# A head over four feature tiles, TensorE without waits for itself, and new paces in a planned attention and feed-forward kernel

## The chip, the cores and the metric

The kernel runs on one core of a Trainium2 chip, as one program. The metric is the time of an execution in microseconds (us); the time of a kernel is the median of its runs. A core has five engines that run beside each other, each through its own instructions in order, with semaphores between them: TensorE (PE) multiplies matrices, VectorE (DVE), ScalarE (ACT) and GpSimd (POOL) do the element work, and SyncE (SP) issues nearly all the DMAs. TensorE writes to PSUM, which has eight banks; one bank holds 128 x 512 values in float32. Everything else is kept in SBUF.

## The reference, cut to what matters

There are 2048 tokens of 640 features. A linear attention with 32 heads of 20 features and a gated feed-forward layer of 1728 hidden features see the same input, and a gate per token mixes them. All inputs are bfloat16.

```python
x = A_x                                        # 1 x 2048 x 640
g = sigmoid((x * gate_w).sum(-1))              # one number per token
q, k, v = heads(x @ wqkv)                      # 32 heads of 20
pq, pk = q @ w_phi, k @ w_phi                  # per head, 20 x 20
phi_q = concat(softmax(pq), softmax(-pq))      # 40 features
phi_k = concat(softmax(pk), softmax(-pk))
kv, z = phi_k.T @ v, phi_k.sum(tokens)
a = ((phi_q @ kv) / (phi_q @ z + 1e-6)) @ wo
b = (silu(x @ w_gate) * (x @ w_up)) @ w_down
out = g * a + (1 - g) * b
```

## The kernel before

**The work.** x is loaded transposed (xT, five chunks of 128 features by 2048 tokens), 512 tokens at a time (bt 0 to 3). The hidden features of the feed-forward layer are cut into 14 tiles of 128 (the last has 64). A gate tile (L658) or up tile (L659) for 512 tokens is five matmuls of 512 columns, one for each chunk, summed in one bank. What follows a pair is `ffn_tail` (L617): ACT takes a tanh of the gate bank into hT and copies the up bank into `us`; DVE combines tanh and gate bank (L636), which frees that bank; POOL multiplies by `us` (L642), of which there are three buffers. hT has two buffers, for bt even and odd. `down` (L744) multiplies 14 tiles of hT by w_down for 128 tokens.

For the attention, `premult` (L766) multiplies w_phi into the q and k weights on TensorE, from block-diagonal weights that POOL builds out of phi's weights (L563 to L574). `features` (L828) makes pq or pk for 128 tokens (ten matmuls into a pair of banks). DVE then takes maxima (L859) and minima (L863), subtracts both (L867, L871; the second one frees the pair), ACT takes the exponential, DVE sums (L882) and inverts (L886), and POOL normalizes (L892). A K tile and its v tile go into `kvpart` (L904) when four K tiles are normalized. Q tiles come after, each with a DMA transpose, a product with kv (`num`), a division, another DMA transpose and the product with wo. `finish` and `finals` (L706, L716) mix both results, and SP writes them out.

**What sets the order.** All of it is entered as tasks in a planner (`_Plan`, L230) that runs when the program is built. A task has an engine, an estimated cost, tasks that it depends on, a rank (`prio`), and banks or buffers that it takes and gives back. The planner simulates the engines: whenever one is free, it takes the task of the lowest rank whose dependencies are done by its estimates, whose buffers are free and whose `hold` time has passed. `after` keeps a task behind another one. A load has a `land` time, its expected landing. The order so found is written into each engine's instructions and does not change when the kernel runs. `K_AT + K_EACH * t` and `Q_AT + Q_EACH * t` are the hold times of the K and Q feature tiles (L840), `PRE_AT` that of the first premultiplication, and `K_PAIRS` tells for how many feature tiles bt 0 and bt 1 take turns in the ranking (L1012).

**Semaphores.** `_Tracker.run` (L161) knows for each tile of SBUF and each PSUM bank the last write and the reads since, and `_emit_waits` (L132) makes the engine wait for those that the new instruction conflicts with, unless they are known to be done. Each task's matmuls count one up on TensorE's own semaphore; a conflict of a matmul with an earlier matmul's write to the same bank is treated like any other, so TensorE waits for its own semaphore.

**The head.** `ffn_head` (L665) starts the feed-forward tiles of bt 0 while their data still comes in. It handles HD = 3 tiles: gate for chunks 0-1, up for chunks 0-1, gate for chunks 2-3, gate for chunk 4 (three tiles in each), and up for chunks 2-4, tile by tile. So six banks are in use. The weights for it come in four loads (`load_head`, L525), between those of x: gate chunks 0-1, x chunks 0-1, up chunks 0-1, gate chunks 2-4, x chunks 2-3, x chunk 4, up chunks 2-4 (L529 to L534). Further weights come in column pieces (`PIECES`, L492). Ahead of the head stands one warm-up task (L596): ten matmuls of 512 and two of 128 columns over all eight banks, whose results nobody reads.

Of the kernel before, what the change touches and what calls it, by code (L numbers as in the profile page):

```python
# [6 lines left out]
P = 128  # L7
# [29 lines left out]
class _Tracker:  # L37
# [94 lines left out]
    def _emit_waits(self, eng, need):  # L132
        kn = self.known[eng]
        eobj = self.engobj[eng]
        while True:
            pending = [(s, v) for s, v in need.items() if v > kn.get(s, 0)]
            if not pending:
                return
            s, v = pending[0]
            eobj.wait_ge(self.sem[s], v)  # L140
            self.nwaits += 1
            if v > kn.get(s, 0):
                kn[s] = v
            snap = self._snap(s, v)
            for s2, v2 in snap.items():
                if v2 > kn.get(s2, 0):
                    kn[s2] = v2
# [13 lines left out]
    def run(self, eng, fn, reads=(), writes=(), semname=None, inc=None):  # L161
        rkeys = [self._key_of(a) for a in reads]
        wkeys = [self._key_of(a) for a in writes]
        need = {}

        def req(ev):
            if ev is None:
                return
            s, v = ev
            if v > need.get(s, 0):  # L170
                need[s] = v

        for k in rkeys:
            for kk in self._conflicts(k):
                req(self.lastw[kk])
        for k in wkeys:
            for kk in self._conflicts(k):
                req(self.lastw[kk])
                for s, v in self.readers[kk].items():
                    req((s, v))  # L180
        self._emit_waits(eng, need)
        ins = fn()
        if semname is None:
            semname = {"pe": "pe", "act": "act", "dve": "dve", "pool": "pool"}[eng]
            if inc is None:
                inc = 1
        elif semname == "dma":
            semname = self.new_dma_sem()
            inc = 16
        ins.then_inc(self.sem[semname], inc)  # L190
        self.cnt[semname] += inc
        v = self.cnt[semname]
        ev = (semname, v)
        snapd = dict(self.known[eng])
        if snapd.get(semname, 0) < v:
            snapd[semname] = v
        self.evknow.setdefault(semname, {})[v] = snapd
        for k in wkeys:
            self.lastw[k] = ev
            self.readers[k] = {}  # L200
        for k in rkeys:
            r = self.readers[k]
            if r.get(semname, 0) < v:
                r[semname] = v
        return ev
# [21 lines left out]
        self.slack = 0.0  # L227


class _Plan:  # L230


# [9 lines left out]
    def add(self, eng, cost, fn, deps=(), prio=5.0, lat=None, acq=(), rel=(), name=""):  # L242
        t = _Task(eng, cost, fn, deps, prio, self.LAT[eng] if lat is None else lat,
                  tuple(acq), tuple(rel), len(self.tasks), name)
        self.tasks.append(t)
        return t
# [86 lines left out]
def _build(  # L333
# [9 lines left out]
    gate_w: bass.AP,  # L343
    out: bass.AP,
):
    tr = _Tracker(nc)
    pe, act, dve, pool, sp = nc.tensor, nc.scalar, nc.vector, nc.gpsimd, nc.sync
    run = tr.run

# [51 lines left out]
    wph = sbat("wph", [P, 5, DH], BF16, base + 10 * D * 2 + 5 * 8 * DH * 2)  # L401

    ps = nc.alloc_psum_tensor("ps", [P, 8 * 512], F32)
# [6 lines left out]
    add = plan.add  # L410
# [4 lines left out]
    def one(b, c0, c1, r0=0, r1=P):  # L415
        return ps[r0:r1, b * 512 + c0:b * 512 + c1]
# [62 lines left out]
    def load(eng, dst, src, land, prio, transpose=False, name="load", cost=0.06):  # L479

        t = add(eng, cost, lambda: dma(eng, dst, src, transpose=transpose), prio=prio, lat=2.0, name=name)
        t.land = land
        t.slack = L_SLACK if land > 13 else 0.0
        t.after = chain.get(eng)
        chain[eng] = t
        return t

    def rows(a):
        return a.rearrange("(c p) j -> p c j", p=P)
    gsrc = rows(B_w_gate)  # L490
    usrc = rows(B_w_up)
    PIECES = ((0, 384), (384, 640), (640, 896), (896, 1280), (1280, 1664))  # L492
    NPC = len(PIECES)
    wgl = [None] * (NPC + 1)
    wul = [None] * (NPC + 1)

    def load_gu(j, eng, land, prio):
        c0, c1 = PIECES[j]
        wgl[j] = load(eng, wg[:, :, c0:c1], gsrc[:, :, c0:c1], land[0], prio)
        wul[j] = load(eng, wu[:, :, c0:c1], usrc[:, :, c0:c1], land[1], prio + 0.1)  # L500

    def load_x(bt, prio, *cuts):

        tok = slice(512 * bt, 512 * bt + 512)
        out_ = []
        for i, (c0, c1, land) in enumerate(cuts):
            out_ += [load("sp", xT[:, c0:c1, tok], x2[tok, c0 * P:c1 * P], land, prio + 0.1 * i, True, "x%d" % bt)] * (c1 - c0)
        return out_

    def load_wT(which, land, prio):  # L510
        o = 5 * which
        return load("sp", wqT[:, o:o + 5, :], A_wqkv[:, which * D:(which + 1) * D], land, prio, True, "wT")
# [6 lines left out]
    gw_l = add("act", 0.5, load_gate, prio=-7, lat=6.0, name="gw")  # L519
    gw_l.hold = 11.0  # L520
    xs = [None] * NBT
    HD = 3
    hw = {}

    def load_head(key, c0, c1, land, prio):  # L525
        w, src = (wg, gsrc) if key == "g" else (wu, usrc)
        hw[key, c0] = load("sp", w[:, c0:c1, 0:HD * P], src[:, c0:c1, 0:HD * P], land, prio)
        return hw[key, c0]
    load_head("g", 0, 2, 3.7, -43)  # L529
    xa = load_x(0, -42, (0, 2, 5.2))  # L530
    load_head("u", 0, 2, 6.0, -41)
    wgl[0] = load_head("g", 2, 5, 7.1, -40.5)
    xs[0] = xa + load_x(0, -40, (2, 4, 8.0), (4, 5, 8.6))
    wul[0] = load_head("u", 2, 5, 9.9, -39)  # L534
    load_gu(1, "sp", (11.2, 12.4), -37)
    ph_l = load("sp", wph[:, :, :], rows(A_w_phi.rearrange("h e f -> (h e) f")), 12.6, -36.5)
    load_gu(2, "sp", (13.8, 15.0), -36)
    xs[1] = load_x(1, -35, (0, 5, 17.5))
    wkT_l = load_wT(1, 20.8, -34)
    load_gu(3, "sp", (22.8, 24.4), -33)  # L540
    wv_l = load("sp", wvg[:, :, 0:D], rows(A_wqkv[:, 2 * D:3 * D]), 27.3, -32)
    xs[2] = load_x(2, -31, (0, 5, 31.0))
    load_gu(4, "sp", (32.4, 33.9), -30)
# [44 lines left out]

    WARM = 10
    wctx = {}

    ones_row = nc.const_aps.tensor(1.0, (P, 512), BF16)

    def warm():  # L596
        def fn():
            for i, n in enumerate([512] * WARM + [P] * 2):
                last = pe.matmul(one(i % 8, 0, n), lhsT=ones_row[:, 0:P], rhs=ones_row[:, 0:n], start=True, stop=True, skip_group_check=True)  # L599
            return last  # L600
        run("pe", fn, reads=[], writes=[ps[:, :]])
    warm_t = add("pe", 0.427 * WARM + 0.2, warm, prio=-10, acq=[("bank", wctx, i) for i in range(8)],
                 rel=[("bank", wctx, i) for i in range(8)], name="warm")


    gate_t = {}
# [3 lines left out]
    def w_dep(k):  # L610
        col = P * k
        for j, (c0, c1) in enumerate(PIECES):
            if col < c1:
# [51 lines left out]
    def ffn_head():  # L665
        tsl = slice(0, 512)
        cs = [{} for _ in range(HD)]
        before = warm_t
        last = {}

        def group(key, c0, c1, by_k=False):
            nonlocal before
            w = wg if key == "g" else wu

            def fn(ks, cc):
                mms([(one(cs[k][key], 0, 512), w[:, c, P * k:P * k + P], xT[:, c, tsl], c == 0, c == 4) for c in cc for k in ks])
            for ks in [(k,) for k in range(HD)] if by_k else [range(HD)]:
                t = add("pe", _mm(*[512] * (len(ks) * (c1 - c0))), lambda ks=ks: fn(ks, range(c0, c1)),
                        deps=[xs[0][c1 - 1], hw[key, min(c0, 2)]], prio=-5,
                        acq=[("bank", cs[k], key) for k in ks] if c0 == 0 else (), name="head")  # L680
                t.after = before
                before = t
                for k in ks:
                    last[key, k] = t
        group("g", 0, 2)
        group("u", 0, 2)
        group("g", 2, 4)
        group("g", 4, 5)
        group("u", 2, 5, by_k=True)
        for k in range(HD):  # L690
            ffn_tail(0, k, cs[k], (last["g", k], last["u", k]), 0)

    B_FIRST = 8
    K_AT, K_EACH, Q_AT, Q_EACH = 29.0, 6.10, 122.4, 7.91
    PRE_Q = 10.08
    PRE_EACH = 2.2
    PRE_AT = 23.7
    D_AFTER = 4
    FIN_DVE = 12
    K_PAIRS = 8  # L700
    store_t = {}
    gs_t = {}
    pend = []
# [297 lines left out]

    pre_k = premult(1, wkT_l, 2.0, at=PRE_AT)
    pre_q = premult(0, wqT_l, PRE_Q, 0.02)
    wq_done[0] = pre_q[-1]
# [9 lines left out]
    for bt in range(1, NBT):  # L1014
        ks = list(range(K_PAIRS if bt == 1 else 0, NK))
# [72 lines left out]
```

## Time and profile before

| | us |
|---|---|
| median of 3 runs | 288.47 |
| lowest, highest | 288.34, 288.76 |
| the profiled execution | 288.7 |
| its span, first to last instruction | 286.9 |
| PE busy | 281.3 |
| DVE busy | 224.0 |
| POOL busy | 171.1 |
| ACT busy | 145.5 |

All rows of the profile come from the one profiled execution, and their times count from the start of its span. The part of its time outside the span is 1.8 us. In a timeline a row is: start, duration, engine, line, operation, tiles (out<-in), shapes, number of instructions, and in brackets the idle time before and what ended it. Matmuls overlap, since each is drawn until its result is out; the spacing of their starts is what the array takes. PEld are the weight loads that belong to the matmuls. All matmuls but the warm-up have line 435 (a helper), so they are told apart by their tiles: wg is gate, wu up, wqk features, wd down. Some matmul records, a few per cent, are missing from the trace. In the view by stretches a row is: start:end, length, busy time and number of instructions of each engine, the granted TensorE clock, the busy share of the DMA engines and the GB/s that they moved.

### The profile page before, as it was taken

The page shows a single profiled execution, that of the slowest core. Times are in us where ns is not written, and L with a number is a line of the kernel's source. Part 1 is how long each engine was busy: PE and PEld are TensorE (multiplying, and loading weights), DVE is VectorE, ACT ScalarE, POOL GpSimd, SP SyncE. Part 2 cuts the span into 40 slices and gives each one's busy share as a digit, 9 for nine tenths or more (in the row PEclk, how much of TensorE's full clock was granted, in tenths as well). Part 3 has the DMA queues.
Part 4 walks back from the last instruction along what each step waited for, and adds up shares of the span by engine and source line. Part 5 has one row for each costly group of instructions (what it writes and reads, how often), then busy time and mean ns, then how long its engine had stood idle before and what let it go on. Part 6 is the DMA issues. An engine that isn't in the chain of part 4 may idle for free.

```text
span 286.9 us, 5145 instructions
## 1 busy us (share of the span) xinstructions
PE 281.3 (98%) x2014; PEld 151.1 (53%) x2052; DVE 224.0 (78%) x318; ACT 145.5 (51%) x222; POOL 171.1 (60%) x164
## 2 busy tenths in 40 slices
PE   8999999999999999999999999999999999999996
PEld 3344555546555545555555555555455565455654
DVE  1233379999999999989999987989999978962212
ACT  2437648676664774445463534456665544562210
POOL 5199305787378656763685566676986666665100
DMA  7999999100000000000118426544346335223211
GB/s 149 265 214 268 258 190 357 58 1 3 0 0 2 0 2 0 2 0 2 26 24 104 104 65 129 72 98 86 84 87 79 75 65 126 46 53 73 72 46 46
DMA packets 65448, 23.91 MB, mean 83 GB/s; under 512 B 53968, under 2 KB 65424, under 8 KB 65424
## 3 DMA queue, kind: packets, MB, share of 16 engines
q1 hardware_dynamic: 64768, 23.58, 38.6%
q8 instruction: 16, 0.26, 0.4%
q10 hardware_dynamic: 656, 0.00, 0.1%
q14 instruction: 8, 0.07, 0.1%
HBM read 8.30 MB, written 2.62 MB: 38 GB/s over the span
## 4 chain that ended last, share of the span: by engine, by line
PE 97%; DVE 1%; issue 1%; DVEq 0%
PE ps L435 95%; PE ps L599 2%; DVE sm L882 1%; DVE mx L859 0%; DVE phi L867 0%; DVE mn L863 0%; DVE xsb L725 0%; DVEq L140 0%
## 5 line engine op out<-in xcount | busy, mean ns | idle before, releaser
L892 POOL TENSOR_TENSOR phi<-phi,rc 128x1320 bf16<-128x1320 bf16 x32 | 77.5, 2423 | 36.9 <-DVE rc L886 36.8
L642 POOL TENSOR_TENSOR hT<-hT,us 128x512 bf16<-128x512 bf16 (+1 forms) x56 | 64.2, 1152 | 35.1 <-DVE hT L636 20.9
L435 PE MATMUL ps<-xT,wg 128*128 128x512 bf16 x272 | 68.2, 380 | 0.9 <-issue 0.2
L435 PE MATMUL ps<-xT,wu 128*128 128x512 bf16 x254 | 63.9, 379 | 0.3
L435 PE MATMUL ps<-wd,hT 128*128 128x128 bf16 (+1 forms) x440 | 62.2, 298 | 0.4
L636 DVE SCALAR_TENSOR_TENSOR hT<-hT,ps 128x512 bf16<-128x512 bf16 (+1 forms) x56 | 37.5, 673 | 22.0 <-ACT hT L445 22.0
L445 ACT ACTIVATE phi<-phi 128x1320 bf16<-128x1320 bf16 x32 | 41.6, 1301 | 22.7 <-DVE phi L871 22.7
L445 ACT ACTIVATE hT<-ps 128x512 bf16<-128x512 f32 (+1 forms) x56 | 33.0, 594 | 38.1 <-PE ps L435 37.8
L882 DVE TENSOR_REDUCE sm<-phi 128x66 f32<-128x1320 bf16 x32 | 48.6, 1519 | 4.7 <-ACT phi L445 4.7
L435 PEld LDWEIGHTS ps<-wd,hT 128*128 128x128 bf16 x448 | 35.0, 98 | 27.1
L435 PE MATMUL ps<-wqk,xT 128*128 128x128 bf16 (+1 forms) x314 | 47.6, 297 | 0.3
L435 PEld LDWEIGHTS ps<-xT,wu 128*128 128x128 bf16 x260 | 25.2, 98 | 31.0 <-issue 1.7
L445 ACT ACTIVATE us<-ps 128x512 bf16<-128x512 f32 (+1 forms) x56 | 33.0, 597 | 15.6 <-PE ps L435 15.5
L435 PEld LDWEIGHTS ps<-xT,wg 128*128 128x128 bf16 x280 | 25.3, 98 | 25.2 <-issue 1.9
L435 PEld LDWEIGHTS ps<-wqk,xT 128*128 128x128 bf16 x320 | 26.2, 98 | 21.2
L859 DVE TENSOR_REDUCE mx<-ps 128x33 f32<-128x660 f32 x32 | 26.8, 837 | 9.5 <-PE ps L435 9.5
L445 ACT ACTIVATE xsb<-ps,gs 128x640 bf16<-128x640 f32 x16 | 12.7, 792 | 30.9 <-PE ps L435 30.9
L871 DVE TENSOR_TENSOR phi<-mn,ps 128x660 bf16<-128x660 f32 x32 | 26.3, 823 | 0.5
L863 DVE TENSOR_REDUCE mn<-ps 128x33 f32<-128x660 f32 x32 | 26.4, 824 | 0.0
L867 DVE TENSOR_TENSOR phi<-ps,mx 128x660 bf16<-128x660 f32 x32 | 26.1, 816 | 0.0
L739 POOL TENSOR_TENSOR xsb<-xsb,xb 128x640 bf16<-128x640 bf16 x12 | 16.7, 1393 | 13.6 <-ACT xb L445 13.6
L435 PE MATMUL ps<-wo,oT 128*128 128x128 bf16 (+1 forms) x155 | 23.4, 296 | 0.3
(44 smaller groups left out, 188.0 us busy)
## 6 DMA issues: line engine op xcount, KB each, us to landing
out_dram<-xsb SPq DMA_DIRECT2D x15, 160.0 KB, 1.8
wd<-in_B_w_down_dram SPq DMA_DIRECT2D x1, 2080.0 KB, 9.6
wg<-in_B_w_gate_dram SPq DMA_DIRECT2D x2, 480.0 KB, 4.3
wu<-in_B_w_up_dram SPq DMA_DIRECT2D x2, 480.0 KB, 5.3
wvg<-in_A_wqkv_dram SPq DMA_DIRECT2D x1, 800.0 KB, 8.1
wo<-in_A_wo_dram SPq DMA_DIRECT2D x1, 800.0 KB, 9.2
wg<-in_B_w_gate_dram SPq DMA_DIRECT2D x2, 320.0 KB, 4.6
wu<-in_B_w_up_dram SPq DMA_DIRECT2D x2, 320.0 KB, 5.2
```

The lines of the kernel that those rows point to most:

```text
L435: last = pe.matmul(o, lhsT=l, rhs=r, start=st, stop=sp_, skip_group_check=True)
L445: run("act", lambda: act.activation(o, i, func, scale=scale), reads=reads, writes=[o])
L599: last = pe.matmul(one(i % 8, 0, n), lhsT=ones_row[:, 0:P], rhs=ones_row[:, 0:n], start=True, stop=True, skip_group_check=True)
L636: dveop(lambda: dve.scalar_tensor_tensor(out=hap, in0=hap, scalar=1.0, in1=g_, op0=ALU.add, op1=ALU.mult), [hap, g_], [hap])
L642: poolop(lambda: pool.tensor_tensor(hap, hap, u_, ALU.mult), [hap, u_], [hap])
L739: poolop(lambda: pool.tensor_tensor(x_, x_, b_, ALU.add), [x_, b_], [x_])
L859: dveop(lambda: dve.tensor_reduce(a, b, AX.X, ALU.max), [b], [a])
L863: dveop(lambda: dve.tensor_reduce(a, b, AX.X, ALU.min), [b], [a])
L867: dveop(lambda: dve.tensor_tensor(o_, a, b, ALU.subtract), [a, mx[:, ctx["st"], :]], [o_])
L871: dveop(lambda: dve.tensor_tensor(o_, a, b, ALU.subtract), [b, mn[:, ctx["st"], :]], [o_])
L882: dveop(lambda: dve.tensor_reduce(a, b, AX.X, ALU.add), [b], [a])
L892: poolop(lambda: pool.tensor_tensor(a, a, b, ALU.mult), [a, r], [a])
```

## The change

1. TensorE's waits for its own semaphore are left out (`_Order`).
2. The head handles four feature tiles (HD = 4), so it uses all eight banks. The gate weights for chunks 2-4 come in two loads, for tiles 0-1 and for tiles 2-3; the second stands behind x chunk 4. The order of the matmuls is: gate chunks 0-1 of four tiles, up chunks 0-1 of four tiles, gate chunks 2-3 and then chunk 4 of tiles 0-1, gate chunks 2-4 of tiles 2-3, up chunks 2-4 tile by tile.
3. The column pieces move along (512, 256, 256, 320, 320 instead of 384, 256, 256, 384, 384), and x of bt 1 is loaded ahead of phi's weights and of the third pieces. The expected landing times are changed.
4. The warm-up has ten matmuls of 512 columns in two tasks, over banks 0-3 and over banks 4-7 (two of them twice).
5. New paces: K_AT, K_EACH, Q_AT, Q_EACH, PRE_Q, PRE_AT, and K_PAIRS 9 instead of 8.

```diff
+class _Order(_Tracker):
+    def _emit_waits(self, eng, need):
+        super()._emit_waits(eng, {s: v for s, v in need.items() if not s == eng == "pe"})
...
-    tr = _Tracker(nc)
+    tr = _Order(nc)
...
-    PIECES = ((0, 384), (384, 640), (640, 896), (896, 1280), (1280, 1664))
+    PIECES = ((0, 512), (512, 768), (768, 1024), (1024, 1344), (1344, 1664))
...
-    HD = 3
+    HD = 4
...
-    load_head("g", 0, 2, 3.7, -43)
-    xa = load_x(0, -42, (0, 2, 5.2))
-    load_head("u", 0, 2, 6.0, -41)
-    wgl[0] = load_head("g", 2, 5, 7.1, -40.5)
-    xs[0] = xa + load_x(0, -40, (2, 4, 8.0), (4, 5, 8.6))
-    wul[0] = load_head("u", 2, 5, 9.9, -39)
-    load_gu(1, "sp", (11.2, 12.4), -37)
-    ph_l = load("sp", wph[:, :, :], rows(A_w_phi.rearrange("h e f -> (h e) f")), 12.6, -36.5)
-    load_gu(2, "sp", (13.8, 15.0), -36)
-    xs[1] = load_x(1, -35, (0, 5, 17.5))
+    load_head("g", 0, 2, 0, HD, 3.9, -43)
+    xa = load_x(0, -42, (0, 2, 5.25))
+    load_head("u", 0, 2, 0, HD, 6.9, -41)
+    load_head("g", 2, 5, 0, 2, 7.4, -40.5)
+    xs[0] = xa + load_x(0, -40, (2, 4, 8.8), (4, 5, 9.3))
+    wgl[0] = load_head("g", 2, 5, 2, HD, 10.0, -39.5)
+    wul[0] = load_head("u", 2, 5, 0, HD, 11.3, -39)
+    load_gu(1, "sp", (12.5, 13.7), -37)
+    xs[1] = load_x(1, -36.5, (0, 5, 16.4))
+    ph_l = load("sp", wph[:, :, :], rows(A_w_phi.rearrange("h e f -> (h e) f")), 16.5, -36.2)
+    load_gu(2, "sp", (17.6, 18.8), -36)
...
-            for i, n in enumerate([512] * WARM + [P] * 2):
-                last = pe.matmul(one(i % 8, 0, n), lhsT=ones_row[:, 0:P], rhs=ones_row[:, 0:n], start=True, stop=True, skip_group_check=True)
+            for b in banks:
+                last = pe.matmul(one(b, 0, 512), lhsT=ones_row[:, 0:P], rhs=ones_row[:, 0:512], start=True, stop=True, skip_group_check=True)
...
+    warm_t = warm((4, 5, 6, 7, 4, 5), warm((0, 1, 2, 3), None))
...
-        group("g", 0, 2)
-        group("u", 0, 2)
-        group("g", 2, 4)
-        group("g", 4, 5)
-        group("u", 2, 5, by_k=True)
+        group("g", 0, 2, [(0, 1, 2, 3)])
+        group("u", 0, 2, [(0, 1, 2, 3)])
+        group("g", 2, 4, [(0, 1)])
+        group("g", 4, 5, [(0, 1)])
+        group("g", 2, 5, [(2, 3)])
+        group("u", 2, 5, [(0,), (1,), (2,), (3,)])
...
-    K_AT, K_EACH, Q_AT, Q_EACH = 29.0, 6.10, 122.4, 7.91
-    PRE_Q = 10.08
+    K_AT, K_EACH, Q_AT, Q_EACH = 30.0, 6.08, 120.8, 8.05
+    PRE_Q = 10.06
...
-    PRE_AT = 23.7
+    PRE_AT = 23.6
...
-    K_PAIRS = 8
+    K_PAIRS = 9
```

More of the change, by code (lines that the diff above doesn't have):

```diff
@@ L521, in _build, with load_head @@
     xs = [None] * NBT
-    HD = 3
+    HD = 4
     hw = {}
-    def load_head(key, c0, c1, land, prio):
+    def load_head(key, c0, c1, k0, k1, land, prio):
         w, src = (wg, gsrc) if key == "g" else (wu, usrc)
-        hw[key, c0] = load("sp", w[:, c0:c1, 0:HD * P], src[:, c0:c1, 0:HD * P], land, prio)
-        return hw[key, c0]
-    load_head("g", 0, 2, 3.7, -43)
-    xa = load_x(0, -42, (0, 2, 5.2))
-    load_head("u", 0, 2, 6.0, -41)
-    wgl[0] = load_head("g", 2, 5, 7.1, -40.5)
-    xs[0] = xa + load_x(0, -40, (2, 4, 8.0), (4, 5, 8.6))
-    wul[0] = load_head("u", 2, 5, 9.9, -39)
-    load_gu(1, "sp", (11.2, 12.4), -37)
-    ph_l = load("sp", wph[:, :, :], rows(A_w_phi.rearrange("h e f -> (h e) f")), 12.6, -36.5)
-    load_gu(2, "sp", (13.8, 15.0), -36)
-    xs[1] = load_x(1, -35, (0, 5, 17.5))
-    wkT_l = load_wT(1, 20.8, -34)
-    load_gu(3, "sp", (22.8, 24.4), -33)
+        t = load("sp", w[:, c0:c1, k0 * P:k1 * P], src[:, c0:c1, k0 * P:k1 * P], land, prio)
+        for k in range(k0, k1):
+            hw[key, c0, k] = t
+        return t
+    load_head("g", 0, 2, 0, HD, 3.9, -43)
[9 more added lines that the diff above has]
+    load_gu(2, "sp", (17.6, 18.8), -36)
+    wkT_l = load_wT(1, 21.6, -34)
+    load_gu(3, "sp", (23.2, 24.8), -33)
     wv_l = load("sp", wvg[:, :, 0:D], rows(A_wqkv[:, 2 * D:3 * D]), 27.3, -32)
@@ L587, in _build, with warm @@
     pad_t = add("pool", 0.7, lambda: memset(phi[:, :, :, GF:P], 0.0, "pool"), prio=2.9, name="pad")
-    WARM = 10
-    wctx = {}
     ones_row = nc.const_aps.tensor(1.0, (P, 512), BF16)
-    def warm():
+    def warm(banks, before):
+        ctx = {}
         def fn():
-            for i, n in enumerate([512] * WARM + [P] * 2):
-                last = pe.matmul(one(i % 8, 0, n), lhsT=ones_row[:, 0:P], rhs=ones_row[:, 0:n], start=True, stop=True, skip_group_check=True)
-            return last
-        run("pe", fn, reads=[], writes=[ps[:, :]])
-    warm_t = add("pe", 0.427 * WARM + 0.2, warm, prio=-10, acq=[("bank", wctx, i) for i in range(8)],
-                 rel=[("bank", wctx, i) for i in range(8)], name="warm")
+            for b in banks:
+                last = pe.matmul(one(b, 0, 512), lhsT=ones_row[:, 0:P], rhs=ones_row[:, 0:512], start=True, stop=True, skip_group_check=True)
+            return last
+        b0, b1 = min(banks), max(banks) + 1
+        t = add("pe", 0.427 * len(banks), lambda: run("pe", fn, reads=[], writes=[ps[:, b0 * 512:b1 * 512]]), prio=-10,
+                acq=[("bank", ctx, i) for i in range(b0, b1)], rel=[("bank", ctx, i) for i in range(b0, b1)], name="warm")
+        t.after = before
+        return t
+    warm_t = warm((4, 5, 6, 7, 4, 5), warm((0, 1, 2, 3), None))
     gate_t = {}
@@ L669, in ffn_head, with group @@
         last = {}
-        def group(key, c0, c1, by_k=False):
+        def group(key, c0, c1, parts):
             nonlocal before
@@ L676, in fn @@
                 mms([(one(cs[k][key], 0, 512), w[:, c, P * k:P * k + P], xT[:, c, tsl], c == 0, c == 4) for c in cc for k in ks])
-            for ks in [(k,) for k in range(HD)] if by_k else [range(HD)]:
+            for ks in parts:
                 t = add("pe", _mm(*[512] * (len(ks) * (c1 - c0))), lambda ks=ks: fn(ks, range(c0, c1)),
-                        deps=[xs[0][c1 - 1], hw[key, min(c0, 2)]], prio=-5,
+                        deps=[xs[0][c1 - 1], hw[key, min(c0, 2), ks[-1]]], prio=-5,
                         acq=[("bank", cs[k], key) for k in ks] if c0 == 0 else (), name="head")
```

## The prediction

> **What bounds the kernel now.** I read the page first: busy shares and the chain that ended last.
>
> ```profile
> PE 281.3 (98%) x2014; PEld 151.1 (53%) x2052; DVE 224.0 (78%) x318; ACT 145.5 (51%) x222; POOL 171.1 (60%) x164
> PE 97%; DVE 1%; issue 1%; DVEq 0%
> ```
>
> TensorE is 98% of the span and 97% of the chain. The number of its matmuls does not change, so only stretches in which TensorE stands still, or does work that counts for nothing, can be won or lost. A matmul that is drawn busy may still wait, so I looked next at the spacing of starts, in the timeline of PE over the first microseconds.
>
> ```profile
> 0.84 4.64 PE L599 MATMUL ps<-const-bfloat16-1.0 128*128 128x512 bf16 x12 [0.84 <-PEq L1072]
> 5.63 1.64 PE L435 MATMUL ps<-xT,wg 128*128 128x512 bf16 x6
> 7.11 1.46 PE L435 MATMUL ps<-xT,wu 128*128 128x512 bf16 x6
> 8.75 1.46 PE L435 MATMUL ps<-xT,wg 128*128 128x512 bf16 x6 [0.18 <-issue]
> 10.36 0.81 PE L435 MATMUL ps<-xT,wg 128*128 128x512 bf16 x3
> 11.00 2.11 PE L435 MATMUL ps<-xT,wu 128*128 128x512 bf16 x9
> 12.94 1.24 PE L435 MATMUL ps<-xT,wg 128*128 128x512 bf16 x5
> 14.02 1.24 PE L435 MATMUL ps<-xT,wu 128*128 128x512 bf16 x4
> ```
>
> The last two rows start 1.08 apart with five matmuls between them (one record is missing in the last row): 0.216 for each 512 columns, with no hole. By that measure the head has holes. Six matmuls from 7.11 would end their issue at 8.41; the next starts at 8.75 (0.34 lost). Six from 8.75 would end at 10.05; the next starts at 10.36 (0.31 lost). From 10.36 it is dense: nine from 11.00 reach 12.94. I call **offset** the start of a matmul less 0.216 times the head matmuls before it; the largest offset in the head is the time that TensorE has lost for good. Now it is 10.36 - 18 x 0.216 = **6.47**.
>
> Which wait ends last at each hole? The timelines of the weight loads (PEld) and of SP, and for each issue the time from issue to landing in the DMA view:
>
> ```profile
> 5.07 0.15 PEld L599 LDWEIGHTS ps<-const-bfloat16-1.0 128*128 128x128 bf16 x1 [0.28 <-issue]
> 5.60 0.14 PEld L435 LDWEIGHTS ps<-xT,wg 128*128 128x128 bf16 x2 [0.39 <-issue]
> 6.01 0.77 PEld L435 LDWEIGHTS ps<-xT,wg 128*128 128x128 bf16 x4 [0.27 <-issue]
> ```
>
> ```profile
> 1.34 1.32 SPq L463 DMA_TRANSPOSE xT<-in_A_x_dram  x1
> 2.71 0.56 SPq L463 DMA_DIRECT2D wu<-in_B_w_up_dram  x1
> ...
> 3.83 2.73 SPq L463 DMA_TRANSPOSE xT<-in_A_x_dram  x2
> 6.61 0.58 SPq L463 DMA_DIRECT2D wu<-in_B_w_up_dram  x1
> 7.23 0.49 SPq L463 DMA_DIRECT2D wg<-in_B_w_gate_dram  x1
> ```
>
> ```profile
> 5.11 1.46 SPq L463 DMA_TRANSPOSE xT<-in_A_x_dram  x1
> ```
>
> ```profile
> xT<-in_A_x_dram SPq DMA_TRANSPOSE x1, 3.6
> wu<-in_B_w_up_dram SPq DMA_DIRECT2D x1, 192.0 KB, 4.1
> xT<-in_A_x_dram SPq DMA_TRANSPOSE x1, 4.8
> xT<-in_A_x_dram SPq DMA_TRANSPOSE x1, 4.1
> wu<-in_B_w_up_dram SPq DMA_DIRECT2D x1, 288.0 KB, 3.5
> wg<-in_B_w_gate_dram SPq DMA_DIRECT2D x1, 320.0 KB, 4.0
> ```
>
> Issue plus time to landing: x chunks 0-1 land at 4.9, up 0-1 at 6.8, x chunks 2-3 at 8.6, x chunk 4 at 9.2, up 2-4 at 10.1, the next gate piece at 11.2. So the first head matmul (5.63) did not wait for x: it waited for the warm-up to finish (0.84 + 4.64 = 5.48). The hole at 8.75 is x chunks 2-3, landed 0.1 before. The hole at 10.36 is no data at all: x chunk 4 had been there for over a microsecond. That group accumulates in the banks that the group before it writes, so the tracker makes TensorE wait for its own last matmul, which ends at 8.75 + 1.46 = 10.21.
>
> **The change part by part.** Rates and cover:
>
> ```profile
> 2.00:3.00 1.00, 1.00 (x4) 0.36 (x3) 0.45 (x3) 0.29 (x2) 0.86 (x4) 1.00 0.72 199
> 9.40:11.50 2.10, 1.95 (x10) 0.78 (x9) 0.00 (x0) 0.30 (x1) 0.00 (x0) 1.00 1.18 301
> 40.00:120.00 80.00, 79.42 (x603) 43.38 (x612) 79.65 (x105) 51.69 (x88) 52.71 (x44) 1.00 0.16 44
> ```
>
> The last figure of each row is GB/s. The DMA engines are the head's supply and are full, so an added byte delays what is behind it: I take 301 GB/s (the stretch of plain weight loads; 64 KB is 0.22) and keep 199 as the other end (0.33).
>
> *Four tiles in the head.* Gate 0-1 and up 0-1 each grow by 64 KB, gate 2-4 and up 2-4 by 96 KB; gate 2-4 is cut in two loads of 192 KB, and only the first goes ahead of x chunks 2-4. I now take each group's data and its offset, with 0.1 from landing to matmul (8.6 to 8.75 above). Before x chunks 2-3 stand 64 + 64 - 96 = +32 KB.
> - gate 0-1: x 4.9 + 0.22 + 0.1 = 5.22. The ten warm-up matmuls are through at 5.07 (the eleventh's weight load), so data, not warm-up, decides.
> - The clock: warm-up matmuls are 0.42 apart ((5.07 - 0.84)/10), the first two head weight loads to the next four 0.38, later ones 0.216. The first head matmul thus lost 0.38 - 0.216 = 0.16; at half rate that is what 0.33 costs, so the rate doubled 0.33 after 5.63, at 5.96. From 5.22 to 5.96 half the time is lost: offset 5.22 + 0.37 = **5.59**.
> - up 0-1: 6.8 + 0.44 + 0.1 = 7.34, after 8 matmuls: 7.34 - 1.73 = **5.61**.
> - gate 2-3 of tiles 0, 1: x 8.6 + 0.11 + 0.1 = 8.81, after 16: 5.35. Its own weights are ahead of x in the queue.
> - gate 4 of tiles 0, 1: 9.2 + 0.11 + 0.1 = 9.41, after 20: 5.09.
> - gate 2-4 of tiles 2, 3: 192 KB (0.65) behind x chunk 4, 10.06, after 22: 5.31.
> - up 2-4: 10.1 + 320 KB (1.09) + 0.1 = 11.29, after 28: 5.24.
> - the next gate piece: 11.2 + 1.09 + 0.1 = 12.39, after 40: 3.75.
>
> The largest is **5.61** against 6.47: **0.86 us won**. The two that set it, the clock and up 0-1, agree by accident. Bounds: at 199 GB/s up 0-1 gives 6.8 + 0.66 + 0.1 - 1.73 = 5.83 (0.64 won); if only the up load's own 64 KB delays it and x is not late, the clock sets it: 5.07 + (5.96 - 5.07)/2 = 5.52 (0.95 won).
>
> *No wait for its own matmuls.* In the head it is the 0.31 above, counted in the offsets. Elsewhere such a wait asks for the previous writer of a bank that another engine has read since, hence long done; from 40 to 120 TensorE is busy 79.42 of 80 with records missing, so I cost it at nothing, gain or loss.
>
> *Warm-up in two tasks, shorter.* Two matmuls of 128 columns go. Worth nothing while x decides the first matmul; without that cover they cost 0.2. No wait is added.
>
> *The moved loads.* One more issue on SP (0.5 to 0.6) and x of the second 512 tokens ahead of phi's weights and two pieces. After the head (40 matmuls, then tiles 4 and 5 from the pieces just priced) TensorE has work until 5.61 + 60 x 0.216 = 18.6. The next pair of rows bounds what is late next.
>
> ```profile
> 10.85 4.70 SPq L463 DMA_TRANSPOSE xT<-in_A_x_dram  x1
> ```
>
> ```profile
> xT<-in_A_x_dram SPq DMA_TRANSPOSE x1, 7.2
> ```
>
> Now x lands at 10.85 + 7.2 = 18.05 with two pieces (656 KB, 2.2) ahead of it; without them and with 1.09 more head it comes near 17, and even the old 18.05 is in time. Behind it POOL's five builds from phi's weights (L567 to L571) move from 13 to about 17:
>
> ```profile
> 12.98 0.30 POOL L567 COPY wbd<-wph 128x140 bf16<-128x140 bf16 x1 [8.31 <-DMA wph<-in_A_w_phi_dram]
> ...
> 18.42 5.77 POOL L642 TENSOR_TENSOR hT<-hT,us 128x512 bf16<-128x512 bf16 x5
> ```
>
> They hold POOL for 5.4 and the products of L642 queue behind them, now as after; TensorE stayed dense across that. Cost nothing; uncovered, up to the 0.9 by which the first premultiplication can be late, with gate and up tiles to fill it.
>
> *New paces.* They reorder the same work. In the stretch of K features VectorE is busy 79.65 of 80: it is full, and TensorE fits around it. I take 0 and bound it by the rivals.
>
> **Sum.** The profiled execution took 288.7 (span 286.9, 1.8 outside it): 288.7 - 0.86 = 287.8. It lies 0.23 above the median 288.47, and nothing in the head says why, so I take the gain from the median: **287.6**.
>
> **Rivals.**
>
> *Given back to VectorE and POOL (no change).* The last kv group, at the end of the K stage:
>
> ```profile
> 129.82 1.52 DVE L882 TENSOR_REDUCE sm<-phi 128x66 f32<-128x1320 bf16 x1
> 131.25 0.84 DVE L867 TENSOR_TENSOR phi<-ps,mx 128x660 bf16<-128x660 f32 x1
> ...
> 132.47 0.78 DVE L871 TENSOR_TENSOR phi<-mn,ps 128x660 bf16<-128x660 f32 x1
> ```
>
> ```profile
> 132.64 2.42 POOL L892 TENSOR_TENSOR phi<-phi,rc 128x1320 bf16<-128x1320 bf16 x1 [3.30 <-DVE rc L886]
> ```
>
> ```profile
> 135.42 0.86 PE L435 MATMUL ps<-v,phi 128*128 128x64 bf16 x24
> ```
>
> POOL's norm ends at 135.06 and kv starts at 135.42 or a weight load earlier: at most 0.36 to spare. If TensorE is 0.86 ahead but VectorE's chain is not, kv waits 0.86 - 0.36 = 0.5 or more, up to the whole 0.86: 288.1 to 288.5. Against it: the paces put one more gate/up pair early (K_PAIRS 9), which can fill the lead.
>
> *The clock or the supply comes late (no change).* Were the rate to double at 6.7 instead of 5.96, the first group's offset would be 5.22 + 0.74 = 5.96 and the gain 0.51: 287.96. Beyond that the kernel before loses alike (its first matmul is at 5.63 and its self-wait of 0.31 stays), so the gain stays near 0.5. [...]
>
> *Slower.* The first Q features may now start at 120.8 of the plan instead of 122.4. If all four VectorE passes of that tile get ahead of the sum at 129.82, instead of two, the sum is late by L867 and L871, 0.84 + 0.78 = 1.62; less 0.36 to spare, TensorE stands 1.26 or more at kv: net +0.4 to +0.8, 288.9 to 289.2. It decides once the stall passes 0.86. Against it: the sum's tile has the earlier rank, so it yields only while its exponential is not done.
>
> **How the numbers follow.** The gain stays: 0.64 (287.5 to 287.85). Given back: 0.15 (288.1 to 288.5). Clock or supply late: 0.08 (287.95). Slower: 0.13 (289.05). A measurement can tell about 0.2% from no change, 0.58 here: faster than 287.89 is 0.65 (the forecast and a little of the third), within 0.22, slower 0.13. The range takes in the first three cases with the spread of the three runs around them (0.13 below, 0.29 above the median): 287.2 to 288.6.
>
> **What would show it.** Right: the first head matmul near 5.2, the ninth near 7.3, no hole at the gate 4 group, and 40 head matmuls ending near 14.3; then PE offsets equal until the end, with the last matmul about 0.86 earlier. Wrong: a hole ahead of up 0-1 over 0.3 (supply), a head that runs beyond 6.5 at 0.42 per matmul (clock), or a start-to-start gap over 0.3 on PE between 20 and 140, ahead of a kv group above all.

## The result, and the profile after

The changed kernel is faster: 287.36 us (median of 7 runs, 287.25 to 287.70) against 288.43 (7 runs, 288.02 to 288.76), a ratio of 0.9967 with a 95% interval of 0.9956 to 0.9979. Two more series on chips of their own, each beside the kernel before, gave 287.81 against 288.50 (0.9971, 0.9961 to 0.9982) and 287.64 against 288.34 (0.9973, 0.9962 to 0.9985). So the gain is 0.7 to 1.1; the forecast was 0.86.

The profiled execution took 287.35, span 285.6. The page's busy line and the chain that ended last:

```profile
PE 282.2 (99%) x2050; PEld 151.0 (53%) x2050; DVE 223.9 (78%) x318; ACT 146.2 (51%) x222; POOL 171.2 (60%) x164
PE 97%; DMA 1%; SPq 0%; DVE 0%; issue 0%
PE ps L442 97%; DMA xT<-in_A_x_dram 1%; SPq L470 0%; DVE xsb L738 0%
```

TensorE is the chain as before, but what stands ahead of it is now the load of x and no longer the warm-up. (L442 is the old L435.) The timeline of PE over the head:

```profile
0.84 4.09 PE L608 MATMUL ps<-const-bfloat16-1.0 128*128 128x512 bf16 x10 [0.84 <-PEq L1085]
5.17 1.89 PE L442 MATMUL ps<-xT,wg 128*128 128x512 bf16 x8 [0.24 <-DMA xT<-in_A_x_dram]
6.90 1.89 PE L442 MATMUL ps<-xT,wu 128*128 128x512 bf16 x8
8.62 2.75 PE L442 MATMUL ps<-xT,wg 128*128 128x512 bf16 x12
11.21 2.75 PE L442 MATMUL ps<-xT,wu 128*128 128x512 bf16 x12
13.80 1.24 PE L442 MATMUL ps<-xT,wg 128*128 128x512 bf16 x5
```

From 5.17 on there is no hole: 8 matmuls to 6.90, 8 to 8.62, 12 to 11.21, 12 to 13.80, each 0.216. The offset is 13.80 - 40 x 0.216 = 5.16, against 6.46 in the profile before. The spans differ by 1.3, and so do these offsets: all of the difference is in the head. The loads behind it, by issue on SP and time from issue to landing (x 0-1, up 0-1, x 2-3):

```profile
1.32 1.32 SPq L470 DMA_TRANSPOSE xT<-in_A_x_dram  x1
2.69 0.57 SPq L470 DMA_DIRECT2D wu<-in_B_w_up_dram  x1
...
3.82 2.53 SPq L470 DMA_TRANSPOSE xT<-in_A_x_dram  x2
```

```profile
xT<-in_A_x_dram SPq DMA_TRANSPOSE x1, 3.7
wu<-in_B_w_up_dram SPq DMA_DIRECT2D x1, 256.0 KB, 3.4
xT<-in_A_x_dram SPq DMA_TRANSPOSE x1, 3.9
```

They land at 5.0, 6.1 and 7.7. The last two are there well ahead of their use, at 6.90 and 8.62; the first one is what the head waits for. Behind the head, the stretch from 40 to 120 and the last kv group of the K stage:

```profile
40.00:120.00 80.00, 80.00 (x616) 43.53 (x614) 79.32 (x104) 50.56 (x84) 53.80 (x45) 1.00 0.16 46
```

```profile
127.06 0.85 DVE L872 TENSOR_REDUCE mx<-ps 128x33 f32<-128x660 f32 x1 [0.21 <-PE ps L442]
127.82 0.83 DVE L876 TENSOR_REDUCE mn<-ps 128x33 f32<-128x660 f32 x1
128.57 1.52 DVE L895 TENSOR_REDUCE sm<-phi 128x66 f32<-128x1320 bf16 x1
```

```profile
131.39 2.43 POOL L905 TENSOR_TENSOR phi<-phi,rc 128x1320 bf16<-128x1320 bf16 x1 [2.54 <-DVE rc L899]
```

```profile
134.18 0.86 PE L442 MATMUL ps<-v,phi 128*128 128x64 bf16 x24
```

kv comes 1.24 earlier than before (135.42), and the sum that it needs comes 1.25 earlier too (129.82). VectorE is as full as it was (79.32 of 80, 79.65 before), yet its whole chain moved along with TensorE. POOL ends at 133.82, and kv has 0.36 to spare, as before.

### The profile page after: what moved, and what is told of

Its sections match the earlier page's. It is cut to its first block, busy times and chain, and to the rows that moved or that the text cites. A ratio compares the mean times of both kernels' runs of the same rounds, so it can differ in the third digit from the quotient of the medians.

```text
span 285.6 us, 5119 instructions
## 1 busy us (share of the span) xinstructions
PE 282.2 (99%) x2050; PEld 151.0 (53%) x2050; DVE 223.9 (78%) x318; ACT 146.2 (51%) x222; POOL 171.2 (60%) x164
## 4 chain that ended last, share of the span: by engine, by line
PE 97%; DMA 1%; SPq 0%; DVE 0%; issue 0%
PE ps L442 97%; DMA xT<-in_A_x_dram 1%; SPq L470 0%; DVE xsb L738 0%
## 5 line engine op out<-in xcount | busy, mean ns | idle before, releaser
L442 PE MATMUL ps<-xT,wg 128*128 128x512 bf16 x280 | 69.1, 379 | 0.2 <-DMA xT<-in_A_x_dram 0.2
L442 PE MATMUL ps<-xT,wu 128*128 128x512 bf16 x260 | 64.3, 379 | 0.0
L442 PE MATMUL ps<-wd,hT 128*128 128x512 bf16 (+1 forms) x448 | 63.0, 299 | 0.0
L442 PEld LDWEIGHTS ps<-wd,hT 128*128 128x128 bf16 x448 | 35.0, 98 | 26.9
L442 PE MATMUL ps<-wqk,xT 128*128 128x512 bf16 (+1 forms) x320 | 48.5, 299 | 0.0
L442 PEld LDWEIGHTS ps<-xT,wu 128*128 128x128 bf16 x260 | 25.3, 98 | 30.9 <-issue 0.3
L442 PEld LDWEIGHTS ps<-xT,wg 128*128 128x128 bf16 x280 | 25.7, 98 | 25.9 <-issue 0.8
L442 PEld LDWEIGHTS ps<-wqk,xT 128*128 128x128 bf16 x320 | 26.2, 98 | 21.2 <-ACT hT L452 0.2
L752 POOL TENSOR_TENSOR xsb<-xsb,xb 128x640 bf16<-128x640 bf16 x12 | 16.7, 1395 | 14.3 <-ACT xb L452 14.3
L442 PE MATMUL ps<-wo,oT 128*128 128x512 bf16 (+1 forms) x160 | 24.3, 299 | 0.0
```

The costliest lines, as they stand in the source:

```text
L442: last = pe.matmul(o, lhsT=l, rhs=r, start=st, stop=sp_, skip_group_check=True)
L752: poolop(lambda: pool.tensor_tensor(x_, x_, b_, ALU.add), [x_, b_], [x_])
```

## The experiments

**Span less offset.** One claim runs through all of them: span = a constant + the largest offset of the head. The offset is the start of the first matmul after the head less 0.216 for each head matmul, from each profile.

| kernel | profiled us | span | offset | span - offset |
|---|---|---|---|---|
| before | 288.70 | 286.94 | 6.46 | 280.48 |
| changed | 287.35 | 285.63 | 5.16 | 280.47 |
| before, again | 288.92 | 287.18 | 6.46 | 280.72 |
| before, no self-waits | 287.94 | 286.22 | 5.80 | 280.42 |
| head alone | 288.64 | 286.92 | 6.27 | 280.65 |
| changed, waits back | 287.95 | 286.23 | 5.70 | 280.53 |
| changed, waits back, again | 287.46 | 285.73 | 5.20 | 280.53 |
| changed, old paces | 287.50 | 285.75 | 5.01 | 280.74 |
| changed, again | 287.89 | 286.15 | 5.68 | 280.47 |
| changed, third | 287.77 | 286.04 | 5.33 | 280.72 |
| gate load by ScalarE | 287.95 | 286.23 | 5.69 | 280.54 |
| x split | 288.78 | 287.07 | 6.59 | 280.48 |
| x split, gate by ScalarE | 287.90 | 286.17 | 5.70 | 280.46 |
| no warm-up | 289.19 | 287.47 | 7.00 | 280.47 |

The offsets spread over 2.0, the last column over 0.32. What is left of that is small holes behind the head, named below. The theory holds; but the offset of one kernel differs between executions by 0.5, so a single profile is a poor measure of a kernel here.

**The kernel before, again.** No edit.

> The kernel before once more, for a second profile. Theory (the head's supply sets the time before): its profiled execution of 288.7 lay 0.27 above its median of 288.43, so in an execution near the median the largest offset of the head is near 6.2 instead of 6.47, with x chunks 2-3 landing near 8.4 instead of 8.6, the self-wait of 0.31 at the gate 4 group unchanged, and no hole after the head. Rival (the difference lies behind the head): offset 6.47 again, and the last matmul differs by other holes.

Its timeline of PE:

```profile
5.63 1.98 PE L435 MATMUL ps<-xT,wg 128*128 128x512 bf16 x6
7.45 1.46 PE L435 MATMUL ps<-xT,wu 128*128 128x512 bf16 x6
8.74 1.46 PE L435 MATMUL ps<-xT,wg 128*128 128x512 bf16 x6
10.35 0.81 PE L435 MATMUL ps<-xT,wg 128*128 128x512 bf16 x3
```

Missed: the execution was slower still (288.92), and its offset the same 6.46, yet for another cause. There is no hole at x chunks 2-3 (7.45 + 6 x 0.216 = 8.75). Instead the first six matmuls took 1.82 for 1.30: their rate, which the prediction calls the clock, doubled about 1.1 after 5.63, and the 0.52 lost there took the place of the hole. The hole of 0.31 at the gate 4 group is as it was. Another 0.25 lies behind the head: the rival is right for that part. The same 0.25 is in the changed kernel's third profile, ahead of a wo group:

```profile
205.39 1.24 PE L442 MATMUL ps<-xT,wu 128*128 128x512 bf16 x5
206.70 1.53 PE L442 MATMUL ps<-wo,oT 128*128 128x512 bf16 x10
```

Five matmuls from 205.39 end their issue at 206.47, and wo starts 0.23 later. The weight loads of that group name the wait:

```profile
206.70 1.36 PEld L442 LDWEIGHTS ps<-wo,oT 128*128 128x128 bf16 x10 [0.56 <-DMA oT<-ob]
```

It is the DMA transpose of oT, in both profiles. The hole is in one of two profiles of the kernel before and in one of three of the changed kernel; what makes the transpose late was not tried.

**TensorE's self-waits.** The changed kernel with them put back, twice, the second time beside the changed kernel:

```diff
-    tr = _Order(nc)
+    tr = _Tracker(nc)
```

> The changed kernel with TensorE's waits for its own matmuls put back, nothing else. Theory: the gate 4 group of tiles 0-1 follows the group that writes the same banks, so TensorE drains once, 0.31 as in the kernel before, and nothing later takes it up, since TensorE is dense from 5.17 on: 287.36 + 0.31 = 287.67 (287.55 to 287.8). Rival (the four-tile head covers the wait, the gain is the wider head alone): 287.36, no hole.

> The changed kernel with the self-waits put back, on the same chip as the changed kernel. Theory: 0.31 above the changed kernel's median of this call (0.2 to 0.45), one hole of 0.31 at the gate 4 group. Rival 1 (covered): the same as the changed kernel. Rival 2 (the first run of this kernel, 288.19, was no accident of the clock): 0.6 or more above, with more than one hole.

> The changed kernel once more, beside the next ones on one chip. Theory: span = 280.4 + the largest offset of the head + holes behind the head, in every kernel; the offset here is 5.1 to 5.2 when the clock has doubled before the first head matmul and grows by half of the time by which it doubles later, so 287.3 to 287.9, median near 287.4. Rival (the first comparison was lucky, the gain is about half): median 287.8 or more.

The first series gave 288.19 (11 runs, ratio to the kernel before 0.9985, 0.9976 to 0.9993), 0.5 more than expected, with no changed kernel beside it. Its profile explains a part: the first eight matmuls took 2.05 for 1.73 (5.07 to 7.12), so the half rate cost 0.32 there, beside the hole of 0.31. In the second it is 288.13 (11 runs, 0.9987, 0.9978 to 0.9996) and the changed kernel 287.81 (8 runs): 0.32 apart, where 0.31 was expected. The single executions overlap (287.46 to 288.43 against 287.40 to 288.00), and the two profiled ones even lie the other way round, so the medians agree with the theory without proving it; the hole in the profile shows it. The PE timeline of the second series' profile:

```profile
4.86 1.89 PE L442 MATMUL ps<-xT,wg 128*128 128x512 bf16 x8 [0.18 <-issue]
6.58 1.89 PE L442 MATMUL ps<-xT,wu 128*128 128x512 bf16 x8
8.31 1.03 PE L442 MATMUL ps<-xT,wg 128*128 128x512 bf16 x4
9.48 1.93 PE L442 MATMUL ps<-xT,wg 128*128 128x512 bf16 x8
```

Four matmuls from 8.31 end their issue at 9.17; the next starts at 9.48. That is the one hole, 0.31. The wider head does not cover it. Behind the head the self-wait costs another 0.06, once: in the kernel before, a gate tile and the up tile after it start 1.14 apart (198.31 and 199.45), in the changed kernel 1.08 (197.07 and 198.15). All five profiles with self-waits have these 0.06, and none of the nine without. The changed kernel, again, was above the forecast in this series (287.81, the rival's bound): x chunks 0-1 landed at 5.5 in its profile, and its offset was 5.68. It was the load that came late, and not the clock, as the theory had it: the eight matmuls from 5.69 took 1.72.

The other way round, the kernel before without self-waits:

```diff
+class _Order(_Tracker):
+    def _emit_waits(self, eng, need):
+        super()._emit_waits(eng, {s: v for s, v in need.items() if not s == eng == "pe"})
...
-    tr = _Tracker(nc)
+    tr = _Order(nc)
```

> The kernel before without TensorE's waits for its own matmuls, nothing else. Theory: the hole of 0.31 at the gate 4 group goes, the first matmul comes about 0.2 earlier, and the hole at x chunks 2-3 stays: 288.43 - 0.31 = 288.12 (288.0 to 288.25). Rival (later work waits for data or for VectorE anyway): 288.43, a hole in the head smaller and another one behind it larger.

```profile
5.35 1.46 PE L441 MATMUL ps<-xT,wg 128*128 128x512 bf16 x6 [0.63 <-DMA xT<-in_A_x_dram]
6.64 1.46 PE L441 MATMUL ps<-xT,wu 128*128 128x512 bf16 x6
8.40 2.10 PE L441 MATMUL ps<-xT,wg 128*128 128x512 bf16 x9 [0.30 <-DMA xT<-in_A_x_dram]
10.34 2.11 PE L441 MATMUL ps<-xT,wu 128*128 128x512 bf16 x9
```

The nine gate matmuls of chunks 2-4 now run through (8.40 + 9 x 0.216 = 10.34); the hole at x chunks 2-3 stays (7.94 to 8.40). The median is 288.23 (11 runs), 0.23 below the kernel before; the ratio 0.9994 (0.9985 to 1.0002) does not exclude no change. So the profile shows the mechanism, and the times alone would not show it.

**The paces.** The changed kernel with the old ones:

```diff
-    K_AT, K_EACH, Q_AT, Q_EACH = 30.0, 6.08, 120.8, 8.05
-    PRE_Q = 10.06
...
-    PRE_AT = 23.6
...
-    K_PAIRS = 9
+    K_AT, K_EACH, Q_AT, Q_EACH = 29.0, 6.10, 122.4, 7.91
+    PRE_Q = 10.08
...
+    PRE_AT = 23.7
...
+    K_PAIRS = 8
```

> The changed kernel with K_AT, K_EACH, Q_AT, Q_EACH, PRE_Q, PRE_AT and K_PAIRS as before, nothing else. Theory (the head's gain stays whatever the paces): 287.36, within 0.15. Rival (the paces keep the lead from being given back): TensorE stands in the K stage, ahead of a kv group or a feature tile, by 0.3 to 0.9: 287.7 to 288.3.

287.83 (12 runs), ratio 0.9974 (0.9965 to 0.9983), beside 0.9967, 0.9971 and 0.9973 of the changed kernel in other series. By the ratios no difference can be told. The median itself missed: it is above 287.36 by more than 0.15 and inside the rival's range. But no changed kernel ran in this series, and its two later medians (287.81, 287.64) are as high.

The profile shows a little of what the rival says. It has 0.27 more behind the head than the changed kernel's first profile (last column of the table), at two places. At 68.6, in the K stage, a v group starts 0.11 late: six premultiplication matmuls from 68.16 last until 68.59, where such a group takes 0.32. And 0.15 is lost ahead of a wo group at 188.78. The first hole is also in the profile of the head alone (below), the other kernel with the old paces and a four-tile head, and in no profile with the new paces. So the new paces may save 0.1, which the medians cannot tell. The head's gain stays with the old paces.

**The head alone.** The kernel before with the head's loads, column pieces and order of matmuls, and with the old waits, warm-up and paces:

```diff
-    HD = 3
+    HD = 4
...
-    load_head("g", 0, 2, 3.7, -43)
+    load_head("g", 0, 2, 0, HD, 3.9, -43)
...
-        group("g", 0, 2)
+        group("g", 0, 2, [(0, 1, 2, 3)])
...
```

> The kernel before with the head over four tiles, its loads and column pieces, and with nothing else of the change: self-waits, the long warm-up and the old paces stay. Theory: the first head matmul waits for the warm-up (5.63 unless the clock doubles early), up 0-1 and x chunks 2-3 come in time, the self-wait of 0.31 stays, so the offset is 5.9 to 6.1 and the time 288.46 - 0.4 = 288.05 (287.8 to 288.3). Rival (the wider head is the whole gain): 287.4.

```profile
0.84 4.64 PE L602 MATMUL ps<-const-bfloat16-1.0 128*128 128x512 bf16 x12 [0.84 <-PEq L1076]
5.63 2.23 PE L435 MATMUL ps<-xT,wg 128*128 128x512 bf16 x8
7.70 1.89 PE L435 MATMUL ps<-xT,wu 128*128 128x512 bf16 x8
9.42 1.03 PE L435 MATMUL ps<-xT,wg 128*128 128x512 bf16 x4
10.60 1.89 PE L435 MATMUL ps<-xT,wg 128*128 128x512 bf16 x8
```

288.19 (11 runs) against 288.50; ratio 0.9993 (0.9984 to 1.0002). The hole at x chunks 2-3 is gone: 16 matmuls of work lie ahead of it instead of 12. But the head waits for the warm-up's end (5.48) and starts at 5.63, the half rate costs 0.34 (8 matmuls take 2.07 for 1.73), and the self-wait costs its 0.31 at 10.29. By this profile the wider head needs the other two edits to pay in full. The medians of this series bear that out for the self-waits only: 288.19 here, 288.13 with the short warm-up and the new paces but with self-waits, 287.81 without them. What the shorter warm-up is worth by itself was not run. The offset of 6.27 is above the 5.9 to 6.1 that was expected, by the half rate; the median is within its range.

**An earlier start.** Three tries to get x chunks 0-1 sooner, beside a third run of the changed kernel for the last two. First, the first gate load from ScalarE's queue, with one warm-up matmul less:

```diff
...
-    load_head("g", 0, 2, 0, HD, 3.9, -43)
-    xa = load_x(0, -42, (0, 2, 5.25))
+    load_head("g", 0, 2, 0, HD, 3.9, -43, "act")
+    xa = load_x(0, -42, (0, 2, 4.7))
...
```

> The changed kernel with the first gate load issued by ScalarE instead of SyncE, so that x chunks 0-1 are issued at once, and with nine warm-up matmuls instead of ten. Theory (the landing of x chunks 0-1 sets the offset): x lands near 4.5 instead of 5.0, the first head matmul comes near 4.7, and the time falls by 0.2 to 0.45 below the changed kernel's median of this call, the less the later the clock doubles. Rival (both loads share the DMA engines, so x lands no earlier): the same time; or the clock takes all of it back.

Time from issue to landing in the DMA view, and the PE timeline:

```profile
xT<-in_A_x_dram SPq DMA_TRANSPOSE x1, 4.0
```

```profile
4.94 2.64 PE L442 MATMUL ps<-xT,wg 128*128 128x512 bf16 x8
7.42 1.89 PE L442 MATMUL ps<-xT,wu 128*128 128x512 bf16 x8
```

287.70 (7 runs) against 287.81: not to be told apart, so the 0.2 to 0.45 did not come. x is issued 0.5 earlier (at 0.80) and lands at 4.8, only some 0.2 earlier than in the changed kernel's first profile: it takes 4.0 instead of 3.7. And in this profile the half rate took the start back: eight matmuls took 2.48 for 1.73.

Then x chunks 0 and 1 in two loads, with gate chunk 0 and gate chunk 1 as two groups and eight warm-up matmuls; and both edits together:

```diff
-    xa = load_x(0, -42, (0, 2, 5.25))
+    xa = load_x(0, -42, (0, 1, 4.4), (1, 2, 5.0))
...
-        group("g", 0, 2, [(0, 1, 2, 3)])
+        group("g", 0, 1, [(0, 1, 2, 3)])
+        group("g", 1, 2, [(0, 1, 2, 3)])
...
```

> The changed kernel a third time, as the measure for the next three on one chip. Theory: 287.4 to 287.8 (the two medians so far), span less the largest offset of the head 280.4 to 280.6 in its profile, whatever the offset is. Rival (something behind the head differs from run to run as well): span less offset outside of that.

> The changed kernel with x chunks 0 and 1 in two loads, gate chunk 0 of four tiles ahead of gate chunk 1 of four tiles, and eight warm-up matmuls. Theory: x chunk 0 lands 0.4 to 0.7 ahead of where both landed, the head begins at 4.4 to 4.6 as soon as the shorter warm-up is done, and each microsecond of earlier start counts half while the clock has not doubled: 0.15 to 0.4 below the changed kernel's median of this call. Rival (one more DMA on SyncE makes x chunk 1 and all behind it later, by 0.3 or more): the same time or slower.

> As the run with x chunks 0 and 1 in two loads, and with the first gate load issued by ScalarE, so that x chunk 0 is SyncE's first issue. Theory: x chunk 0 lands near 4.0, the warm-up's end (4.25) decides the first head matmul, 0.2 to 0.45 below the changed kernel's median of this call. Rival (the gate load, wanted too, is then the later one, or the clock takes it back): within 0.1 of the run with x split alone.

The changed kernel gave 287.64 (6 runs), the split 288.70 (11 runs; ratio to the kernel before 1.0011, 1.0001 to 1.0021), both edits 288.08 (11 runs; 0.9989, 0.9980 to 0.9998). The split is 1.06 slower than the changed kernel. Its issues on SP and its PE timeline:

```profile
1.33 2.52 SPq L470 DMA_TRANSPOSE xT<-in_A_x_dram  x2
3.90 0.59 SPq L470 DMA_DIRECT2D wu<-in_B_w_up_dram  x1
```

```profile
4.78 1.91 PE L442 MATMUL ps<-xT,wg 128*128 128x512 bf16 x8 [0.75 <-DMA xT<-in_A_x_dram]
7.18 1.90 PE L442 MATMUL ps<-xT,wu 128*128 128x512 bf16 x8 [0.49 <-DMA wu<-in_B_w_up_dram]
9.42 1.46 PE L442 MATMUL ps<-xT,wg 128*128 128x512 bf16 x6 [0.34 <-DMA xT<-in_A_x_dram]
11.34 1.47 PE L442 MATMUL ps<-xT,wg 128*128 128x512 bf16 x6 [0.46 <-DMA wg<-in_B_w_gate_dram]
```

The rival is right, and larger than it said. Two transposing loads of one chunk hold SP for 2.52, where one of two chunks holds it for 1.32. So up 0-1 is issued at 3.90 instead of 2.69, and the loads behind it are issued 1.2 to 1.5 later. That makes three holes, ahead of up 0-1, x chunks 2-3 and the gate weights of tiles 2-3, where the changed kernel has none. The start gained 0.4. With the gate load moved to ScalarE the holes shrink (idle time of 0.24 ahead of up 0-1 and 0.27 ahead of the gate weights of tiles 2-3, none at x chunks 2-3), but both its theory and its rival missed: x chunk 0 landed at 4.6 and not near 4.0, the head began at 4.74, and the median is 0.44 above the changed kernel's and 0.62 below the split's. No version here is faster than the changed kernel by more than can be told. The third profile of the changed kernel has a last column of 280.72, so the rival holds there: the hole ahead of wo, above, differs from run to run as well.

**No warm-up.** The head's first task follows nothing:

```diff
-    warm_t = warm((4, 5, 6, 7, 4, 5), warm((0, 1, 2, 3), None))
+    warm_t = None
```

> The changed kernel without any warm-up matmul, nothing else. [...] Rival (the clock doubles at a time that the first matmul does not set): within 0.5 of the changed kernel.

```profile
5.00 3.57 PE L442 MATMUL ps<-xT,wg 128*128 128x512 bf16 x8 [5.00 <-DMA xT<-in_A_x_dram]
8.36 2.26 PE L442 MATMUL ps<-xT,wu 128*128 128x512 bf16 x8
10.46 2.75 PE L442 MATMUL ps<-xT,wg 128*128 128x512 bf16 x12
```

289.38 (10 runs, 288.74 to 290.75; ratio 1.0039, 1.0027 to 1.0052), 1.74 above the changed kernel, so the rival missed. Eight matmuls take 3.36 (0.42 each), the next eight 2.10, then 0.216 each: the rate doubled near 9.1, 4.1 after the first matmul, which starts at 5.00. In the 13 profiles with a warm-up, where the first matmul starts at 0.84 or 0.85, it had doubled by 3.5 to 6.7, so its moment moved with TensorE's first matmul. The offset of 7.00 follows, and all ten executions are slower than every one of the changed kernel in this series (288.15 at most). In the kernel before without self-waits the rate doubled 2.9 after the first matmul.

## Why the prediction was right, point by point

- *What bounds the kernel.* Right. TensorE's dense stream has a fixed length, and only the head's holes count; the table shows it for 14 profiles.
- *The self-wait, 0.31.* Right: 0.31 in the five profiles that have it, and 0.32 between two medians of one series. Elsewhere it was costed at nothing, and it is 0.06.
- *The offset before, 6.47.* The same in the second profile, but by another sum (half rate instead of x chunks 2-3). A typical execution lies lower: both profiled ones were 0.3 to 0.5 above the medians (288.70 to 288.43, 288.92 to 288.46). That makes the two first profiles differ by 1.30, and the medians by 0.7 to 1.1.
- *Added bytes delay what is behind them* (0.22 for 64 KB, 0.44 at up 0-1). Not borne out. From issue and time to landing, x chunks 0-1 land at 5.0, 5.5 and 5.2 in the three profiles of the changed kernel, at 4.9 and 5.5 in the two of the kernel before; up 0-1, a third larger, lands at 6.1, 6.5 and 6.0 against 6.8 and 6.3. The landings of one load differ by 0.5 between executions, and the added bytes are lost in that. What the DMA engines moved was no constant of 301 either: from 2.70 to 6.10 it was 258, 237 and 270 GB/s in those three profiles, and 194 and 217 in the two of the kernel before. So the term 5.61 of up 0-1 never decided: in the three profiles the largest offset was that of x chunks 0-1 (5.16, 5.68, 5.33).
- *The clock, 0.37.* Right in that matmuls start at half rate (0.427 for 512 columns, 0.216 later) and wrong as a constant; that it is the clock was not shown, since the granted-clock column says 1.00 from 0.84 to 15 in the profiles before and after. In the three profiles of the changed kernel the rate had doubled by the time of the first head matmul and cost nothing; so the ninth matmul came at 6.90 in the first of them where 7.3 was forecast, and the head ended at 13.80 instead of 14.3. It cost 0.32 with the waits back, 0.34 in the head alone and 0.75 with the gate load on ScalarE. The reading of the kernel before was slightly short: its first six matmuls lost 0.18 (1.48 for 1.30) and not 0.16, which puts the doubling at 6.0 and not 5.96. Its moment, from TensorE's first matmul, was between 2.7 (x split, whose eighth warm-up matmul starts at 3.65 instead of 3.78) and 5.9 (the kernel before, again).
- *Loads moved, POOL's builds later, paces: nothing.* Right within what can be told. TensorE is 80.00 of 80 busy between 40 and 120, and the old paces give the same time but for the 0.1 above.
- *Given back to VectorE and POOL.* Did not happen. The rival took VectorE's chain to be fixed in time; it moved by 1.25 with TensorE. With the old paces that sum comes as early (128.53), so the new paces are not what moved it. A busy share of 99% (79.32 of 80) did not mean that it set the pace.
- *Slower by Q's passes.* Did not happen: two passes, not four, stand ahead of the sum at 128.57.

That the total came so near is partly luck, because two wrong sizes cancel: the offset after was forecast at 5.61 and was 5.16 to 5.68, and the offset before, taken from an execution slower than the median, was too high as well.

## What to carry to other kernels

Where one engine's stream is dense to the end, add up where it stands before it becomes dense: the largest of (landing of a group's data less the work ahead of that group) is what the head costs, and only an edit that lowers that largest term pays (in the 14 profiles here span less offset stays within 280.42 to 280.74). An engine's waits for its own last instruction are worth removing where consecutive groups share a bank (0.31 here); behind the head all the others together cost 0.06 in this kernel. Profile such a kernel more than once before sizing its terms, since landings alone moved the changed kernel's offset by 0.5 between executions (5.16 to 5.68), and landings and the half rate that of the one with waits back by as much (5.20 and 5.70).

## What the runs showed of the hardware

TensorE's first matmuls ran at half rate (0.427 from start to start for 512 columns, 0.216 later), and the rate doubled 2.7 to 5.9 after the first of them, at no fixed moment (5.2 and 5.9 after, in the two profiles of the kernel before). The granted-clock column says 1.00 from 0.84 to 15 in the profiles before and after (also from 2 to 3 in the kernel before, where starts are 0.42 apart), so the doubling is read from the spacing of starts. It came later where the first matmul did (near 9.1 without a warm-up, first matmul at 5.00); what brings it about was not shown.

A transposing load held SP's queue nearly as long with one chunk of 512 tokens (1.21 and 1.26 in the split, 2.52 for the pair) as with two (1.32); with five it was 4.70. Cutting the load of two chunks in two, to get the first half early, made all that is issued behind it 1.2 or more later.

Up 0-1 at 256 KB landed no later after its issue (3.4 in the changed kernel) than at 192 KB (4.1 before), with the DMA engines about full at the time (busy share 1.09 from 3 to 5 in the changed kernel, 0.98 before).
